# Causal attention and a cosine MoE layer on one core: k arrives in 32 by 32 blocks, VectorE turns them

## The chip, the core and the metric

The kernel runs on one core of a Trainium2 chip. The core has TensorE (PE in the rows: matmuls and transposes; PEld are its weight loads), VectorE (DVE), ScalarE (ACT), GpSimd (POOL) and SyncE (SP), which here only issues DMAs; its rows are marked SPq. 16 DMA engines move the data between HBM and SBUF. Matmuls write to PSUM, which here is eight banks of 128 x 512 numbers. The metric is the device time of one execution in microseconds (us). A profile is one more execution, with its own time.

## What is computed

```python
def _attn_ref(q, k, v):                      # each (4, 12, 448, 64), float32
    scale = 1.0 / np.sqrt(q.shape[-1])
    scores = scale * np.matmul(q, k.transpose(0, 1, 3, 2))
    mask = np.triu(np.ones((seq, seq), dtype=bool), k=1)
    scores = np.where(mask, -1000000000.0, scores)
    scores = scores - np.max(scores, axis=-1, keepdims=True)
    attn = np.exp(scores)
    attn = attn / (np.sum(attn, axis=-1, keepdims=True) + 1e-09)
    return np.matmul(attn, v)

def _moe_ref(x, w_in, w_out):                # x (1792, 768): heads side by side
    h = x @ w_in                             # w_in (768, 2048), float64
    g = h * np.cos(h)
    return g @ w_out                         # w_out (2048, 768), float64
```

## The kernel before

It has two stages. **Attention** takes the first 165 us or so and works on 24 pairs of heads (4 batches, 6 pairs each). The MoE layer follows, with products of numbers split into a high and a low half; the change doesn't touch it, but its input is attention's output, and its first weights are loaded and split in small pieces beside the attention.

Of a pair the 448 positions are three blocks of 128 and a tail of 64. q and k come as they lie in memory, positions on partitions, the two heads side by side in 128 columns (`load_qk`; `qn`, `kn`: three buffers each, the rows' `land`). The two tails of q are put on partitions 0 to 63 and 64 to 127, each in its own columns, so that one matmul serves the tails of both heads. TensorE transposes q and k, four 128 x 128 transposes each, to a PSUM bank (`transpose_qk`, line 319), and ScalarE copies each bank to SBUF (`evac_qk`, lines 329 and 331; the rows' `flat`); for k with the factor 1/8. Then TensorE makes the scores: main blocks at line 348, the tail at 357. VectorE adds the mask, negates, takes the row minimum and writes it all to SBUF (`masked`, line 365); ScalarE makes the exponentials and their sums (379); VectorE the reciprocals (390, 391), GpSimd the products (397). TensorE transposes the probabilities (419, tail 429), four banks of them, which two copies of VectorE (541, 543) and two of ScalarE (550, 552) bring to SBUF (`pm`). TensorE multiplies them with v (443), and ScalarE and VectorE split the result into halves (459, 463).

The order is written out by hand in one loop (`for i in range(N + 3)`), and every engine works its own list in that order. Step i makes the scores of pair i, transposes q and k of pair i + 1, finishes the probabilities of pair i - 1 and multiplies v of pair i - 2. At its head SyncE issues the loads of q and k of pair i + 2 and of v of pair i + 1: ten DMAs, two for the main part of each of q, k, v (one per head, lines 240), two for q's tails (258), one each for the tails of k and v (246). ScalarE issues k of the first two pairs; all the rest is SyncE's. On the same queue, behind them, stand the DMAs of the weight pieces (lines 112, 117, 195, 197, 1336), about one per step. A load waits for a semaphore that says that its buffer is free, and for another that says that the DMA eight places ahead of it has landed.

Of the kernel before, what the change touches and what calls it, by code (L numbers as in the profile page):

```python
# [15 lines left out]
AF = mybir.ActivationFunctionType  # L16
ALU = mybir.AluOpType
# [4 lines left out]
def kernel(  # L22
# [27 lines left out]
    NEG = -1.0e9  # L50
# [168 lines left out]
    def attention(filler):  # L219
        with (  # L220
# [4 lines left out]
                "p (t c d) -> p t c d", c=NB + 1, d=P  # L225
            )
            qn_t = [rows[:, i] for i in range(3)]
            kn_t = [rows[:, 3 + i] for i in range(3)]
            vn_t = [cst.tile([P, NB + 1, P], F32, name=f"vn{i}") for i in range(4)]
            pl_t = [cst.tile([P, (NB + 1) * P], F32, name=f"pl{i}") for i in range(2)]  # L230
            pairs = [(b, hp) for b in range(B) for hp in range(NP)]
            N = len(pairs)
            nat, qkt, prob, ptr = {}, {}, {}, {}
# [4 lines left out]
            def load_main(dst, src, b, h0, eng=nc.sync):  # L238
                for j in range(2):
                    eng.dma_start(  # L240
                        out=dst[:, 0:NB, heads(j)],
                        in_=src[b, h0 + j, 0 : NB * P, :].rearrange("(c p) d -> p c d", p=P),
                    )

            def load_tail(dst, src, b, h0, eng=nc.sync):
                eng.dma_start(
                    out=dst[0:TAIL, NB, :].rearrange("p (h d) -> p h d", h=2),
                    in_=src[b, h0 : h0 + 2, NB * P : S, :].rearrange("h p d -> p h d"),
                )

            def load_qk(i, keng=nc.sync):
                b, hp = pairs[i]
                qn = qn_t[i % 3]
                kn = kn_t[i % 3]
                load_main(qn, q, b, 2 * hp)
                load_main(kn, k, b, 2 * hp, keng)
                for j in range(2):
                    nc.sync.dma_start(
                        out=qn[heads(j), NB, heads(j)], in_=q[b, 2 * hp + j, NB * P : S, :]
                    )  # L260
                load_tail(kn, k, b, 2 * hp, keng)
                nat[i] = [qn, kn]

            warm = cst.tile([P, P], BF16, name="warm")
# [1 line left out]

            for i in range(3):
                nc.vector.memset(qn_t[i][:, NB, :], 0.0)
                nc.vector.memset(kn_t[i][TAIL:P, NB, :], 0.0)
                if i == 0:  # L270
                    load_qk(0, nc.scalar)

                    nc.scalar.copy(cst.tile([P, 32], BF16, name="tab")[:, 0:1], warm[:, 0:1])
                elif i == 1:
                    load_qk(1, nc.scalar)
            wps = new_bank()

            def keep_warm(n):
# [9 lines left out]
            nc.gpsimd.memset(trif, 0.0)  # L288
            nc.gpsimd.affine_select(
                out=trif, in_=trif, pattern=[[-1, P]], base=0, channel_multiplier=1,  # L290
                compare_op=ALU.is_ge, fill=NEG,
            )
            mask = cst.tile([P, NB * P], F32, name="mask")
            mask_t = cst.tile([P, S], F32, name="mask_t")
# [17 lines left out]

            def transpose_qk(i, which):
                src = nat[i][which]
                pt = new_bank()
                for c in range(NB + 1):
                    nc.tensor.transpose(pt[:, c * P : (c + 1) * P], src[:, c, :], ident)
                qkt[i, which] = pt  # L320

            def evac_qk(i, which, dve=False):
                pt = qkt[i, which]
                w = (NB * P + P, S)[which]
                t = flat[:, 2 * which + i % 2, 0:w]
                if dve:
                    nc.vector.tensor_scalar(t, pt[:, 0:w], (1.0, scale)[which], None, op0=ALU.mult)
                elif which == 0:
                    nc.scalar.copy(t, pt[:, 0:w])
                else:  # L330
                    nc.scalar.activation(t, pt[:, 0:w], AF.Copy, scale=scale)
                qkt[i, which] = t

            OFF = [c * (c + 1) // 2 * P for c in range(NB + 1)]

# [27 lines left out]
            def masked(dst, src, m, st, n):  # L363

                nc.vector.tensor_tensor_reduce(  # L365
                    out=dst, in0=src, in1=m, scale=-1.0, scalar=3.0e38,
                    op0=ALU.add, op1=ALU.min, accum_out=st[:, 0, n : n + 1],
                )

# [29 lines left out]
            def normalise_block(i, c):  # L399
                pb, _, st = prob[i]  # L400
                normalise(pb[:, :, OFF[c] : OFF[c] + (c + 1) * P], st, slice(2 * c, 2 * c + 2))
# [71 lines left out]
            LOW = [(0, 0, P), (1, P, 2 * P)]  # L473
            TOP = [(2, 0, 3 * P)]
            load_v(0)
            transpose_qk(0, 1)
            evac_qk(0, 1)
            transpose_qk(0, 0)
            evac_qk(0, 0, dve=True)
            keep_warm(7)  # L480
            LO, TL = slice(0, 4), slice(TAILC, TAILC + 1)
            av_of = {}
            for i in range(N + 3):
                cur, prev, nxt = i < N, 0 < i <= N, i + 1 < N
                old, done = 0 <= i - 2 < N, 0 <= i - 3 < N
                if i + 2 < N:
                    load_qk(i + 2)
                if nxt:
                    load_v(i + 1)
                if cur:  # L490
                    open_scores(i)
                    pb, pl, st = prob[i]
                    top = scores_main(i, TOP)
                    low = scores_main(i, LOW)
                    if i == 0:
                        transpose_qk(1, 1)
                        transpose_qk(1, 0)
                    tail = scores_tail(i)
                if nxt and i:
                    transpose_qk(i + 1, 0)  # L500
                    transpose_qk(i + 1, 1)
                if prev:
                    inverse(i - 1, LO)
                    normalise_block(i - 1, 0)
                    normalise_block(i - 1, 1)
                if cur:
                    for j in range(2):
                        masked_block(i, top, 2, j, 0)
                if prev:
                    inverse(i - 1, TL)  # L510
                    normalise(prob[i - 1][1][:, 0:S], prob[i - 1][2], TL)
                if cur:
                    for j in range(2):
                        exp_block(i, 2, j)
                if done:
                    finish_hi(i - 3, av_of[i - 3])
                if cur:
                    for c in range(2):
                        for j in range(2):
                            masked_block(i, low, c, j, c * P)  # L520
                        if (i, c) == (0, 0):
                            evac_qk(1, 1, dve=True)
                            evac_qk(1, 0)
                    masked(pl[:, 0:S], tail[:, 0:S], mask_t, st, TAILC)
                if nxt and i:
                    evac_qk(i + 1, 0)
                    evac_qk(i + 1, 1)
                if cur:
                    for j in range(2):
                        exp_block(i, 0, j)  # L530
                    inverse(i, slice(4, 6))
                    normalise_block(i, 2)
                if done:
                    finish_lo(i - 3, av_of.pop(i - 3))
                if N <= i < N + 2:
                    fill(3 * NCC)
                if prev:
                    open_ptr(i - 1)
                    pm = pm_of(i - 1)
                    t = tp_blocks(i - 1, [(2, kc, j) for kc in range(2) for j in range(2)])  # L540
                    nc.vector.tensor_copy(pm[:, 0:2, :, 2 * P : 3 * P], quad(t))
                    t = tp_blocks(i - 1, [(c, c, j) for c in (0, 2) for j in range(2)])
                    nc.vector.tensor_copy(
                        ptr[i - 1].rearrange("p (a r) -> p a r", a=2)[:, :, 0 : 2 * S].rearrange(
                            "p a (h s) -> p a h s", h=2
                        )[:, :, :, 0:P],
                        quad(t),
                    )
                    t = tp_blocks(i - 1, [(1, kc, j) for kc in range(2) for j in range(2)])
                    nc.scalar.copy(pm[:, 0:2, :, P : 2 * P], quad(t))  # L550
                    t = tp_tail(i - 1)
                    nc.scalar.copy(
                        pm[:, :, :, NB * P : S], t.rearrange("p (k h t) -> p k h t", k=NB + 1, h=2)
                    )
                if cur:
                    for j in range(2):
                        exp_block(i, 1, j)
                    exp(pl[:, 0:S], st, TAILC)
                if old:
                    av_of[i - 2] = av(i - 2)  # L560
                if i == N + 1:
                    run(filler)
                yield i
# [824 lines left out]
```

## Time and profile before

| | |
|---|---|
| median of 3 runs | 629.23 us (629.19 to 631.29) |
| profiled execution | 629.1 us |
| its span, first to last instruction | 627.3 us |
| busy in the span: PE / PEld | 618.9 us (99%) / 542.9 (87%) |
| DVE / ACT / POOL | 481.5 (77%) / 426.7 (68%) / 437.6 (70%) |
| TensorE's granted clock | 1.000 |
| DMA packets / under 512 bytes | 125004 / 73072 |

The shares are means over two unlike stages. Matmuls are pipelined, so a busy PE says that there is always one under way, not that it is at its peak. SyncE has no line in the list of busy times, since issuing isn't counted as busy; what it does is read from the timeline. Idle time of an engine that isn't the bottleneck costs nothing.

### The profile page before, as it was taken

What the parts mean: (1) busy time and instruction counts of PE and PEld (TensorE: products, weight loads), DVE (VectorE), ACT (ScalarE), POOL (GpSimd) and SP (SyncE); (2) the same over time, 40 slices, a digit from 0 to 9 for tenths busy, and PEclk for the clock granted to TensorE, in tenths of its full rate; (3) what the DMA queues carried; (4) which work ended last, traced back from release to release, by engine and by line L of the source; (5) the groups of instructions that cost most, each with busy time, mean ns of one, the idle gap of its engine ahead of it and who ended that gap; (6) DMA issues with size and microseconds to landing.
All of it is one profiled execution on the core that took longest, in us unless ns stands there. A gap on an engine that the chain in (4) does not pass through costs nothing.

```text
span 627.3 us, 11479 instructions
## 1 busy us (share of the span) xinstructions
PE 618.9 (99%) x3705; PEld 542.9 (87%) x3705; DVE 481.5 (77%) x1078; ACT 426.7 (68%) x951; POOL 437.6 (70%) x432
## 2 busy tenths in 40 slices
PE   8999999999999999999999999999999999999997
PEld 6676767677679888999999999999999999999996
DVE  6988888888838678878777777774458877887887
ACT  4998999899877668877777877743346545644640
POOL 2656665666524868877778778782578788788885
PEclk9999999999999999999999999999999999999999
DMA  5645655557604777968697969669997577559204
GB/s 121 144 113 129 159 122 139 146 133 186 175 9 130 243 291 204 376 224 325 220 328 228 340 199 340 238 239 367 401 401 266 158 245 260 184 164 317 84 1 152
DMA packets 125004, 133.29 MB, mean 212 GB/s; under 512 B 73072, under 2 KB 109280, under 8 KB 124944
## 3 DMA queue, kind: packets, MB, share of 16 engines
q1 hardware_dynamic: 117328, 106.23, 53.8%
q0 software_dynamic: 4928, 24.78, 10.9%
q10 hardware_dynamic: 2688, 1.54, 0.8%
q8 instruction: 30, 0.49, 0.3%
q14 instruction: 30, 0.25, 0.1%
HBM read 82.58 MB, written 49.94 MB: 211 GB/s over the span
## 4 chain that ended last, share of the span: by engine, by line
PE 62%; DVE 0%; issue 0%; DVEq 0%
PE banks L667 18%; PE banks L1105 12%; PE banks L1085 12%; PE banks L572 5%; PE banks L573 5%; PE banks L571 5%; PE banks L1122 2%; PE banks L1009 2%; DVE ct L176 0%; DVE acc L655 0%; DVE r L581 0%; DVE acc L1132 0%; DVEq L1132 0%
## 5 line engine op out<-in xcount | busy, mean ns | idle before, releaser
L655 DVE TENSOR_TENSOR acc<-acc,banks 128x768 f32<-128x768 f32 (+1 forms) x122 | 112.7, 932 | 44.4 <-PE banks L667 34.1
L667 PE MATMUL banks<-w,gh 128*128 128x384 f32 x512 | 109.9, 335 | 0.6 <-DVE acc L655 0.3
L397 POOL TENSOR_TENSOR pb<-pb,stat 128x768 f32<-128x768 f32 (+2 forms) x72 | 74.0, 1042 | 43.1 <-DVE stat L391 18.9
L667 PEld LDWEIGHTS banks<-w,gh 128*128 128x128 f32 x512 | 90.7, 188 | 2.6 <-DVE acc L655 0.8
L379 ACT ACTIVATE pb<-pb,stat 128x384 f32<-128x384 f32 (+1 forms) x144 | 72.5, 511 | 17.2 <-DVE stat L365 17.2
L571 PE MATMUL banks<-xa,w 128*128 128x512 f32 x192 | 75.0, 391 | 0.0
L573 PE MATMUL banks<-xa,w 128*128 128x512 f32 x192 | 75.0, 391 | 0.0
L572 PE MATMUL banks<-xa,w 128*128 128x512 f32 x192 | 75.0, 390 | 0.0
L667 PE MATMUL banks<-w,gl 128*128 128x384 f32 x256 | 65.1, 335 | 0.0
L689 POOL TENSOR_TENSOR w<-ct,w 128x768 fp32r<-128x768 f32 x28 | 51.9, 1854 | 16.8 <-ACT w L688 14.2
L365 DVE CUSTOM_DVE_ANT_0 pb<-banks,mask 128x384 f32<-128x384 f32 (+1 forms) x144 | 53.0, 418 | 12.4 <-PE banks L348 12.4
L579 ACT ACTIVATE ni<-banks 128x512 int32<-128x512 f32 (+1 forms) x64 | 34.5, 539 | 34.7 <-PE banks L573 20.8
L598 POOL TENSOR_TENSOR gl<-r,gh 128x512 fp32r<-128x512 f32 x32 | 41.5, 1298 | 19.3 <-ACT gh L597 19.2
L581 DVE SCALAR_TENSOR_TENSOR r<-ni,banks 128x512 f32<-128x512 int32 (+1 forms) x56 | 35.0, 625 | 20.3 <-ACT ni L579 19.7
L443 PE MATMUL banks<-pm,vn 128*64 128x448 f32 (+3 forms) x384 | 46.8, 386 | 0.4
L583 ACT ACTIVATE r<-r 128x512 f32<-128x512 f32 (+1 forms) x56 | 32.8, 586 | 20.9 <-DVE r L581 20.5
L667 PEld LDWEIGHTS banks<-w,gl 128*128 128x128 f32 x256 | 46.4, 188 | 0.0
L443 PEld LDWEIGHTS banks<-pm,vn 128*64 128x64 f32 x384 | 25.5, 136 | 23.2 <-issue 13.0
L586 DVE SCALAR_TENSOR_TENSOR r<-r,banks 128x512 f32<-128x512 f32 (+1 forms) x56 | 35.0, 625 | 13.1 <-ACT r L584 13.1
L1085 PE MATMUL banks<-xb,bb 128*128 128x384 f32 x234 | 44.7, 334 | 0.0
L1105 PE MATMUL banks<-big,gh 128*128 128x384 f32 x168 | 42.7, 335 | 0.0
L573 PEld LDWEIGHTS banks<-xa,w 128*128 128x128 f32 x192 | 36.0, 188 | 7.6
(151 smaller groups left out, 1555.9 us busy)
## 6 DMA issues: line engine op xcount, KB each, us to landing
bb<-w_in_d SPq DMA_DIRECT2D x48, 384.0 KB, 5.1
land<-in_moe_w_in_dram SPq DMA_DIRECT2D x14, 768.0 KB, 5.4
land<-in_moe_w_out_dram SPq DMA_DIRECT2D x14, 768.0 KB, 5.6
w_out_d<-w POOLq DMA_DIRECT2D x14, 768.0 KB, 5.4
big<-w_out_d SPq DMA_DIRECT2D x25, 384.0 KB, 4.5
w_in_d<-w POOLq DMA_DIRECT2D x7, 768.0 KB, 4.3
raw_d<-ct POOLq DMA_DIRECT2D x14, 384.0 KB, 7.7
land<-in_q_dram SPq DMA_DIRECT2D x48, 96.0 KB, 2.7
```

The source lines that it names most:

```text
L365: nc.vector.tensor_tensor_reduce(out=dst, in0=src, in1=m, scale=-1.0, scalar=3.0e38, op0=ALU.add, op1=ALU.min, accum_out=st[:, 0, n : n + 1],)
L379: nc.scalar.activation(dst, dst, AF.Exp, scale=-1.0, bias=st[:, 0, n : n + 1], accum_out=st[:, 1, n : n + 1],)
L397: nc.gpsimd.tensor_tensor(dst, dst, r.to_broadcast(list(dst.shape)), op=ALU.mult)
L443: nc.tensor.matmul(o[heads(j), kc * P : S], lhsT=vn[:, kc, heads(j)], rhs=pm[:, kc, j, kc * P : S], start=(kc == 0), stop=(kc == NB),)
L571: yield nc.tensor.matmul(hv, lhsT=wh[:, f], rhs=x[:, 0, cc, t], start=(cc == 0), stop=False)
L572: yield nc.tensor.matmul(hv, lhsT=wh[:, f], rhs=x[:, 1, cc, t], start=False, stop=False)
L573: yield nc.tensor.matmul(hv, lhsT=wl[:, f], rhs=x[:, 0, cc, t], start=False, stop=(cc == NCC - 1))
L655: nc.vector.tensor_tensor(d, d, o, op=ALU.subtract)
L667: nc.tensor.matmul(o[:, e, 0:EH], lhsT=a[:, cs], rhs=w[:, e * EH : (e + 1) * EH], start=(x == 0), stop=(x == 5),)
L689: nc.gpsimd.tensor_tensor(w[:, 1], tf, f32(w[:, 0]), op=ALU.subtract)
L1085: nc.tensor.matmul(o, lhsT=w[:, u, k * P : (k + 1) * P], rhs=x[k][:, v], start=k + m == 0, stop=k == K - 1 and m == 2,)
L1105: nc.tensor.matmul(o[:, b % 2, 0:EH], lhsT=g_ops[i][u][:, c * P : (c + 1) * P], rhs=wouts[g, i][:, v], start=(x == 0), stop=(x == 2),)
```

## The change

Of k only the way to its transposed form changes. Memory is read in blocks of 32 columns: for each head and each half of its 64 columns one DMA takes all 448 positions, 32 on partitions and 14 groups of them along the row, in runs of 32 numbers (128 bytes). A transpose instruction of VectorE turns each 32 x 32 block in place, and with the blocks so laid out the result is k transposed, heads one above the other, in the same `flat` buffer that the evacuation wrote before. TensorE's transposes of k and ScalarE's evacuations of k go. The factor 1/8 moves to the scale of the mask's pass, and the mask's fill is divided by it. One of VectorE's two copies of probabilities goes to ScalarE. The clearing of k's unused rows goes, since there are none.

```diff
-            kn_t = [rows[:, 3 + i] for i in range(3)]
+            kn_t = [rows[:, 3 + i].rearrange("p c d -> p (c d)")[:, 0:S] for i in range(3)]
...
-                load_main(kn, k, b, 2 * hp, keng)
+                for j in range(2):
+                    for d in range(D // TR):
+                        p = j * D + d * TR
+                        keng.dma_start(
+                            out=kn[p : p + TR].rearrange("r (a c) -> r a c", c=TR),
+                            in_=k[b, 2 * hp + j, :, d * TR : (d + 1) * TR].rearrange(
+                                "(a r) c -> r a c", r=TR
+                            ),
+                        )
...
-                load_tail(kn, k, b, 2 * hp, keng)
...
+            def transpose_k(i):
+                t = qkt[i, 1] = flat[:, 2 + i % 2, 0:S]
+                nc.vector.transpose(t, nat[i][1])
...
-                    out=dst, in0=src, in1=m, scale=-1.0, scalar=3.0e38,
+                    out=dst, in0=src, in1=m, scale=-scale, scalar=3.0e38,
...
                     normalise_block(i - 1, 1)
+                if nxt and i:
+                    transpose_k(i + 1)
                 if cur:
                     for j in range(2):
                         masked_block(i, top, 2, j, 0)
...
-                    nc.vector.tensor_copy(
+                    nc.scalar.copy(
                         ptr[i - 1].rearrange("p (a r) -> p a r", a=2)[:, :, 0 : 2 * S].rearrange(
```

SyncE's list, one step in the middle of attention, before (`land` is q's or k's buffer; the sizes are those of the destination, x2 says twice in a row):

```order
L240 DMA land<-in_q_dram 128x3x64 x2
L240 DMA land<-in_k_dram 128x3x64 x2
L258 DMA land<-in_q_dram 64x64 x2
L246 DMA land<-in_k_dram 64x2x64
L240 DMA vn_90<-in_v_dram 128x3x64 x2
L246 DMA vn_90<-in_v_dram 64x2x64
```

The same place after:

```order
L241 DMA land<-in_q_dram 128x3x64 x2
L260 DMA land<-in_k_dram 32x14x32 x4
L267 DMA land<-in_q_dram 64x64 x2
L241 DMA vn_90<-in_v_dram 128x3x64 x2
L247 DMA vn_90<-in_v_dram 64x2x64
```

Two main pieces and a tail of k have become four equal pieces, ahead of q's tails: eleven DMAs in place of ten.

VectorE's list from the end of one step to the masks of the next, before (`ISA` at line 365 is the mask's pass):

```order
L541 COPY pm<-banks 128x4x128
L543 COPY pm<-banks 128x2x2x128
L143 SCALAR_TENSOR_TENSOR ct<-st,ct 128x256
L147 SCALAR_TENSOR_TENSOR ct<-st,ct 128x256
L390 TENSOR_SCALAR stat<-stat 128x4
L391 RECIPROCAL stat<-stat 128x4
L365 ISA pb,stat<-banks,mask 128x384
```

The same place after:

```order
L543 COPY pm<-banks 128x4x128
L143 SCALAR_TENSOR_TENSOR ct<-st,ct 128x256
L147 SCALAR_TENSOR_TENSOR ct<-st,ct 128x256
L394 TENSOR_SCALAR stat<-stat 128x4
L395 RECIPROCAL stat<-stat 128x4
L336 STREAM_TRANSPOSE flat<-land 128x448
L369 ISA pb,stat<-banks,mask 128x384
```

The second copy is gone from here, and the transpose of the next pair's k stands between the reciprocal and the first mask pass of the present pair. On TensorE the eight transposes of a step at line 319 have become four.

## Rows read from the trace of the kernel before

**Rows 1.** Busy time by stretch: span, engines (x instructions), clock, DMA share.

```profile
core 0: us, PE busy (x) PEld busy (x) DVE busy (x) ACT busy (x) POOL busy (x), PEclk, DMA share, GB/s
90.00:120.00 30.00, 29.93 (x234) 21.58 (x233) 26.25 (x116) 27.35 (x89) 18.41 (x20) 1.00 0.61 147
```

**Rows 2.** Timeline of TensorE, one pair's period: start, length, what.

```profile
87.96 1.57 PE L348 MATMUL banks<-flat 64*128 64x384 f32 x12
...
90.31 1.04 PE L319 MATMUL banks<-ident,land 128*128 128x128 f32 x8
91.19 1.47 PE L419 MATMUL banks<-ident,pb 128*128 128x128 f32 x12
...
96.41 1.02 PE L357 MATMUL banks<-flat 128*128 128x448 f32 x2
97.26 1.04 PE L319 MATMUL banks<-ident,land 128*128 128x128 f32 x8
```

**Rows 3.** Timeline of SyncE, one pair's loads and the next issue.

```profile
132.00 1.12 SPq L240 DMA_DIRECT2D land<-in_q_dram  x2
133.16 1.02 SPq L240 DMA_DIRECT2D land<-in_k_dram  x2
134.22 1.13 SPq L258 DMA_DIRECT2D land<-in_q_dram  x2
135.40 0.62 SPq L246 DMA_DIRECT2D land<-in_k_dram  x1
136.12 1.07 SPq L240 DMA_DIRECT2D vn<-in_v_dram  x2
...
138.00 0.55 SPq L1336 DMA_DIRECT2D raw_d<-ct  x1
```

**Rows 4.** The same timeline: pair 4's loads, two long issues, weights, pair 23's loads.

```profile
21.24 1.08 SPq L240 DMA_DIRECT2D land<-in_q_dram  x2
...
62.98 2.10 SPq L240 DMA_DIRECT2D land<-in_k_dram  x2
...
78.32 2.12 SPq L258 DMA_DIRECT2D land<-in_q_dram  x2
...
152.85 0.38 SPq L195 DMA_DIRECT2D w_out_d<-w  x1
153.29 0.44 SPq L117 DMA_DIRECT2D st<-in_moe_w_out_dram  x1
153.78 1.08 SPq L240 DMA_DIRECT2D land<-in_q_dram  x2
```

**Rows 5.** DMA queues from 60 to 150 us: packets, MB, share of 16 engines.

```profile
q1 hardware_dynamic: 39700, 12.86, 59.2%
q8 instruction: 6, 0.10, 0.4%
```

**Rows 6.** Instructions of line 246: ns at the least, median, at the most.

```profile
L246 SPq DMA_DIRECT2D land<-in_k_dram x22: 621/622/1528, 11.5 to 158.2; - x22
```

**Rows 7.** Waits of SyncE, 30 to 170 us: total, times, longest.

```profile
SPq L246 <- PE banks L348: 6.0, 15, 0.9
```

**Rows 8.** Last pair: SyncE's timeline, tails' landing (median, from the DMA view), TensorE's timeline.

```profile
158.20 0.62 SPq L246 DMA_DIRECT2D land<-in_k_dram  x1
...
land<-in_k_dram SPq DMA_DIRECT2D x13, 32.0 KB, 2.2
...
160.53 1.04 PE L319 MATMUL banks<-ident,land 128*128 128x128 f32 x8
```

**Rows 9.** Instruction groups by line and form, 10 to 190 us: busy, mean ns.

```profile
L543 DVE COPY pm<-banks 128x512 f32<-128x512 f32 x24 | 16.3, 680 | 0.0
L365 DVE CUSTOM_DVE_ANT_0 pl<-banks,mask_t 128x448 f32<-128x448 f32 x24 | 14.9, 620 | 0.0
L550 ACT COPY pm<-banks 128x512 f32<-128x512 f32 x24 | 14.0, 582 | 3.0 <-PE banks L419 2.8
L331 ACT ACTIVATE flat<-banks 128x448 f32<-128x448 f32 x22 | 12.1, 552 | 0.0
```

More of the change, by code (lines that the diff above doesn't have):

```diff
@@ L227, in attention @@
             qn_t = [rows[:, i] for i in range(3)]
-            kn_t = [rows[:, 3 + i] for i in range(3)]
+            kn_t = [rows[:, 3 + i].rearrange("p c d -> p (c d)")[:, 0:S] for i in range(3)]
             vn_t = [cst.tile([P, NB + 1, P], F32, name=f"vn{i}") for i in range(4)]
             pl_t = [cst.tile([P, (NB + 1) * P], F32, name=f"pl{i}") for i in range(2)]
+            TR = 32
             pairs = [(b, hp) for b in range(B) for hp in range(NP)]
@@ L268, in attention @@
                 nc.vector.memset(qn_t[i][:, NB, :], 0.0)
-                nc.vector.memset(kn_t[i][TAIL:P, NB, :], 0.0)
                 if i == 0:
@@ L290, in attention @@
                 out=trif, in_=trif, pattern=[[-1, P]], base=0, channel_multiplier=1,
-                compare_op=ALU.is_ge, fill=NEG,
+                compare_op=ALU.is_ge, fill=NEG / scale,
             )
@@ L311, in load_v, with transpose_q @@
                 nat[i].append(vn)
-            def transpose_qk(i, which):
-                src = nat[i][which]
+            def transpose_q(i):
+                src = nat[i][0]
                 pt = new_bank()
@@ L319, in transpose_qk, with evac_q @@
                     nc.tensor.transpose(pt[:, c * P : (c + 1) * P], src[:, c, :], ident)
[L320 to L332, printed above, removed]
+                qkt[i, 0] = pt
+            def evac_q(i):
+                t = flat[:, i % 2]
+                nc.scalar.copy(t, qkt[i, 0])
+                qkt[i, 0] = t
+            def transpose_k(i):
+                t = qkt[i, 1] = flat[:, 2 + i % 2, 0:S]
+                nc.vector.transpose(t, nat[i][1])
             OFF = [c * (c + 1) // 2 * P for c in range(NB + 1)]
@@ L475, in attention @@
             load_v(0)
[L476 to L479, printed above, removed]
+            transpose_k(0)
+            transpose_q(0)
+            evac_q(0)
             keep_warm(7)
@@ L495, in attention @@
                     if i == 0:
-                        transpose_qk(1, 1)
-                        transpose_qk(1, 0)
+                        transpose_q(1)
                     tail = scores_tail(i)
                 if nxt and i:
-                    transpose_qk(i + 1, 0)
-                    transpose_qk(i + 1, 1)
+                    transpose_q(i + 1)
                 if prev:
@@ L521, in attention @@
                         if (i, c) == (0, 0):
-                            evac_qk(1, 1, dve=True)
-                            evac_qk(1, 0)
+                            transpose_k(1)
+                            evac_q(1)
                     masked(pl[:, 0:S], tail[:, 0:S], mask_t, st, TAILC)
                 if nxt and i:
-                    evac_qk(i + 1, 0)
-                    evac_qk(i + 1, 1)
+                    evac_q(i + 1)
                 if cur:
```

## Prediction

> **What bounds the kernel now.** I read the busy time by stretch first. In the attention stage, where the change lies, TensorE is busy without a break, while ScalarE has 27.35 and VectorE 26.25 us of a 30 us stretch [rows 1]. The timeline of TensorE gives its period: a pair's transposes of q and k begin at 90.31 and the next pair's at 97.26, so 6.95 us for a pair, and the eight transposes take 0.88 of it, 0.11 each [rows 2]. That alone says: take four of eight away and a pair costs 6.51.
>
> But one row of the profile isn't counted as an engine: SyncE, which issues the loads. Its timeline [rows 3] shows a pair's ten loads one right behind the other: two for the main part of q from 132.00 to 133.16, two for k (1.06 us), two tails of q (1.18), the tail of k (0.72), then v; 6.00 us from q to the next piece of work. On top come the DMAs of the weights, 20 in the 19 pairs between 21.24 and 153.78, at 0.44 us and more, and stops of about 1 us: at 62.98 two issues that take 1.02 elsewhere took 2.10, at 78.32 two that take 1.13 took 2.12 [rows 3, 4]. They come about every 15 us, as do the packets of the queue that fetches instructions (6 in 90 us) [rows 5]. All together 132.54 us for 19 pairs, 6.98 us each [rows 4]: just what TensorE needs. The issue times repeat to the nanosecond: 621 at the least and 622 in the median for the 22 tails of k [rows 6]. So I read them as the sequencer's own work and not as waits, though the waits view puts some of them down to TensorE, 15 at this line [rows 7]: that engine's semaphore moves all the time, and a wait would scatter. What shows that SyncE doesn't run ahead is the lead: the tail of k of the last pair is issued at 158.20, a tail lands after 2.2 us, so at 160.4, and TensorE begins with that pair's transposes at 160.53 [rows 8]. **Two queues are full at once**: TensorE and SyncE's issue, and SyncE can't store up a lead.
>
> **The change, part by part.** *k's transposes leave TensorE.* Four of eight, 4 x 0.11 = 0.44 us a pair, on the path as long as TensorE sets the pace. 22 pairs in the steady part make 9.7 us. This is the most that can be gained.
>
> *Copies change sides.* VectorE loses the copy at line 543, 0.68 us, and gets one transpose of 128x448; none is in the trace. Ends: the cheap one is a little under the 0.62 of its other pass over 448 columns, the dear one twice that [rows 9]. I take 0.6. Its load of 26.25/30 x 6.95 = 6.08 us a pair then stays at 6.0, or 6.7 at the dear end. ScalarE loses the evacuation of k at line 331 (0.55) and gets a copy like line 550 (0.58): 27.35/30 x 6.95 = 6.34 becomes 6.37. Both lie under 6.51, so at nothing, covered by TensorE or SyncE; without that cover ScalarE's 6.37 would be next. The factor in the mask's pass changes an operand only, and three memsets ahead of the loop go: nothing.
>
> *k's loads on SyncE.* Three issues become four, each of 32 rows by 14 blocks of 32 numbers. Descriptors double (896 to 1792 a pair), but the issue time doesn't follow their number: a main piece of 384 rows of 256 bytes takes 1.06/2 = 0.53 us, a tail of q of 64 such rows 1.18/2 = 0.59, the tail of k of 128 of them 0.72 [rows 3]. No row shows a 32-row issue, so bounds: the cheapest issue that stands in a queue, 152.85 to 153.29 for a weight's store, is 0.44 [rows 4], the dearest the tail of k, 0.72. What k costs now is 1.06 + 0.72 = 1.78 a pair. Four at 0.44 are 1.76 (-0.02), at 0.53 2.12 (+0.34), at 0.59 2.36 (+0.58), at 0.72 2.88 (+1.10). Both kinds with fewer than 128 partitions are dearer than the main piece, and the new ones have fewer still and, as the tail of k, three dimensions; so I take 0.65, between the two tails: 2.60, **+0.82 us a pair**. A gain below zero I exclude but for the 0.02: it would need an issue under 0.44, and the queue has none that is behind another.
>
> *What waits for that.* The queue is in order, so the tails of q, then v, then the weights' DMAs all move back by it, and the next pair's loads behind them. TensorE's new slack can't help: its transposes of q, and now VectorE's transpose of k, wait for landings. SyncE goes from 6.98 to 7.80 us a pair, TensorE would need 6.51: SyncE sets the end of the stage, and the 0.44 us turns into idle time of TensorE.
>
> *Where the transpose stands.* It is moved ahead of the mask passes of the current pair, behind the first reciprocal. VectorE now waits there for k; queued behind it are the masked maxima, which ScalarE's exponentials wait for. TensorE reads k some 2.8 us into a pair's period (scores begin at 87.96, q's and k's transposes at 90.31, and q's four take 0.44 [rows 2]); VectorE wants it about at its start. Against that k's last piece is no longer behind q's two tails, 1.18 us. Once the pace is SyncE's, this is paid a single time, not per pair: 2.8 - 1.18 = 1.6 less what the earlier start of the masks still finds idle on VectorE, say 0.9; and the last pair, after which SyncE has no more loads, still saves its 0.44. Together +0.5.
>
> **Sum.** The loads of pairs 2 to 23 go over SyncE; 21 of them lie ahead of the last: 21 x 0.82 = 17.2, and 0.5. The profiled execution took 629.1 us (span 627.3 and 1.8 around it), and the median of the runs, 629.23, is the same within 0.1. 629.1 + 17.7 = 646.8. All behind the attention stage moves back by the same amount, since the next stage begins with attention's output. By the bounds: 629.1 + 21 x (-0.02) + 0.5 = 629.2; with 0.53, 636.7; with 0.72, 652.7; and if the first tail of q behind a small piece gets dearer too, by the 0.13 between the tails, 655.
>
> **Rivals.** *TensorE keeps the pace* (faster). It needs SyncE to have room that I don't see: small issues at about 0.33 us, so that four cost 0.47 less than 1.78 now and the period falls to 6.51, or a part of today's issue times that are waits after all. Then 629.1 - 9.7 = 619.4, and with ScalarE at 6.37 under a pace of 6.51 a few waits in each pair: 620. For it: most of the issues do carry a wait. Against it: the repeated times and the lead of 0.1 us at the last pair. The Trainium skill is on this side: its page "DMA: Bandwidth & Descriptors", section "Issuing engines are not separate DMA queues", says that the time to initiate a DMA on a sequencer is usually small beside the DMA itself. By it a fourth issue would be free and the sum 620. The trace doesn't agree for this queue: 0.53 us of issue beside a landing of 2 to 3 us, but ten in a row in a period of 6.98.
>
> *SyncE keeps its pace as it is* (no change). The new pieces cost what the cheapest does, 0.44; TensorE's gain falls into the wait for loads: 629 to 631.
>
> *The DMA engines become the bound* (slower than my forecast). They are 59.2% busy now, with 39700 packets in 90 us on 16 engines, so 21.5 ns a packet [rows 5]. Twice k's packets at that price add 896 x 21.5 / 16 = 1.2 us of 6.95, a share of 0.77: no bound. The other packets of a pair take 0.592 x 16 x 6.98 - 896 x 21.5 ns = 46.8 us of the engines; a period of 7.80 has 125, so k's 1792 packets would have to take over 43 ns each. At 50 the period is 8.5 us: 629.1 + 21 x 1.55 = 662. The skill's same page, "Specifications", puts line rate at 512 bytes and more, with a read-modify-write below; k's rows go from 256 to 128 bytes, both below. By it this rival's chance, which is within the 0.06, would be more, but no row has a packet of 128 bytes.
>
> **Chances.** SyncE's issue sets a longer pace (636 to 655): 0.72; it keeps the present one (629 to 632): 0.11; TensorE keeps the pace (around 620): 0.11; the engines or something else, over 655: 0.06. The first is the forecast: 647. The first two hold 0.83, so the range goes from 629 to 655. Half a percent is 3.1 us, about what can be told from no change: faster 0.11, same 0.12, slower 0.77.
>
> **What would show it.** On SyncE's timeline, four issues of k back to back at 0.53 to 0.72 us, and q to q 7.3 to 8.1 us apart. TensorE with idle time of over a microsecond in each pair, ahead of the four transposes of q or of the scores, ended by DMA, VectorE or ScalarE. VectorE idle ahead of its transpose, ended by the load of k. ScalarE's and VectorE's busy time a pair nearly as before. The MoE stages unchanged in length. Wrong it is if SyncE shows gaps while TensorE still runs at 6.5, if the small issues take under 0.45, or if the granted clock of TensorE, 1.00 now [rows 1], falls with the idle time and TensorE itself gets longer.

## The result, and the profile after

The changed kernel takes 637.47 us (median of 4 runs, 637.07 to 637.99); the kernel before took 629.21 in the same comparison (4 runs, 628.66 to 631.29). The ratio is 1.0126, with an interval of 1.0101 to 1.015: slower by 8.3 us. The forecast was 647, slower by 17.7.

The profiled execution's span is 635.4 us, before 627.3: 8.1 more. First the stretch of [rows 1] again, from the busy time by stretch (columns as there):

```profile
core 0: us, PE busy (x) PEld busy (x) DVE busy (x) ACT busy (x) POOL busy (x), PEclk, DMA share, GB/s
60.00:90.00 30.00, 28.21 (x209) 18.38 (x209) 26.39 (x103) 26.56 (x83) 18.38 (x19) 1.00 0.67 146
90.00:120.00 30.00, 28.89 (x218) 18.99 (x216) 26.16 (x103) 26.70 (x87) 17.68 (x19) 1.00 0.63 140
```

TensorE, busy for 29.93 of 30 us before, now has idle time, and no other engine has taken its place. The granted clock is 1.00 as before. The engine that isn't in these columns is SyncE; its timeline (start, length, what), with the same places as [rows 3, 4]:

```profile
21.96 1.07 SPq L241 DMA_DIRECT2D land<-in_q_dram  x2
...
131.10 0.98 SPq L241 DMA_DIRECT2D land<-in_q_dram  x2
132.12 2.05 SPq L260 DMA_DIRECT2D land<-in_k_dram  x4
134.21 1.13 SPq L267 DMA_DIRECT2D land<-in_q_dram  x2
135.44 1.06 SPq L241 DMA_DIRECT2D vn<-in_v_dram  x2
136.59 0.63 SPq L247 DMA_DIRECT2D vn<-in_v_dram  x1
137.27 1.12 SPq L241 DMA_DIRECT2D land<-in_q_dram  x2
...
161.81 1.10 SPq L241 DMA_DIRECT2D land<-in_q_dram  x2
165.04 1.13 SPq L267 DMA_DIRECT2D land<-in_q_dram  x2
```

The four pieces of k stand from 132.12 to 134.21, 2.09 us or 0.52 each; k cost 1.78 before. The two tails of q behind them take 1.23 (134.21 to 135.44), 1.18 before. From pair 4 to pair 23 SyncE needs 161.81 - 21.96 = 139.85 us, 7.36 for a pair, before 6.98 [rows 4]. That is +0.38, of which the rows above give 0.31 + 0.05. Pair 23's loads begin 161.81 - 153.78 = 8.03 us later than before, and the span is 8.1 longer: **the whole loss can be read off SyncE's list**. That list has no room: between 30 and 160 us never more than 0.44 us lies between the end of one issue and the start of the next. Nor does a load wait there for the one eight places ahead of it: each of the 220 DMAs issued from 25 to 160 us starts at least 0.99 us after that one has landed (both worked out from this trace). That the list is the cause, and not a picture of another engine's pace, is for the experiments to show.

That the loads have no lead is seen at the last pair. TensorE's timeline, with the idle time and its releaser in brackets:

```profile
166.94 0.49 PE L326 MATMUL banks<-ident,land 128*128 128x128 f32 x3
167.90 0.30 PE L326 MATMUL banks<-ident,land 128*128 128x128 f32 x1 [0.47 <-DMA land<-in_q_dram]
```

The three main blocks of q are transposed, and the tail, issued behind 165.04, has not landed. In the middle of the stage the wait goes around by k. VectorE's timeline, and then ScalarE's:

```profile
91.50 0.18 DVE L395 RECIPROCAL stat<-stat 128x4 f32<-128x4 f32 x1
92.13 0.65 DVE L336 STREAM_TRANSPOSE flat<-land 128x448 f32<-128x448 f32 x1 [0.46 <-DMA land<-in_k_dram]
92.70 0.52 DVE L369 CUSTOM_DVE_ANT_0 pb<-banks,mask 128x384 f32<-128x384 f32 x1
```

```profile
93.33 0.62 ACT L383 ACTIVATE pb<-pb,stat 128x384 f32<-128x384 f32 x1 [1.09 <-DVE stat L369]
```

VectorE stands before its transpose until k has landed, the first mask pass starts behind it, and ScalarE waits 1.09 us for that mask's minimum. Read alone, ScalarE's line would blame VectorE; VectorE's line names the load. Over the stage, from the waits between 20 and 165 us (total, times, longest):

```profile
ACT pb L383 <- DVE stat L369: 18.9, 20, 1.9
...
DVE flat L336 <- DMA land<-in_k_dram: 6.4, 10, 1.3
...
PE banks L326 <- DMA land<-in_q_dram: 3.1, 4, 1.4
```

The new operations by line and form, 10 to 190 us, beside [rows 9] (busy, mean ns, idle before):

```profile
L552 ACT COPY pm<-banks 128x512 f32<-128x512 f32 x24 | 14.2, 592 | 0.1
L336 DVE STREAM_TRANSPOSE flat<-land 128x448 f32<-128x448 f32 x22 | 14.2, 646 | 7.6 <-DMA land<-in_k_dram 7.5
```

And the DMA queue from 60 to 150 us, beside [rows 5]:

```profile
q1 hardware_dynamic: 49553, 12.08, 61.7%
```

A quarter more packets in the same time, and the engines' share went from 59.2% to 61.7%. The MoE stage has not changed, it starts later: in the chain that ended last a block of 48 of its products takes 8.4 us in both, at 245.50 before and 253.61 after.

```profile
245.50 8.46 PE banks L667 x48
```

```profile
253.61 8.42 PE banks L669 x48
```

### The profile page after: what moved, and what is told of

Read it like the earlier page. It is cut to its first block, busy times and chain, and to the rows that moved or that the text cites. A ratio compares the mean times of both kernels' runs of the same rounds, so it can differ in the third digit from the quotient of the medians.

```text
span 635.4 us, 11342 instructions
## 1 busy us (share of the span) xinstructions
PE 614.5 (97%) x3609; PEld 530.1 (83%) x3609; DVE 487.5 (77%) x1073; ACT 428.4 (67%) x953; POOL 437.3 (69%) x432
## 4 chain that ended last, share of the span: by engine, by line
PE 61%; DVE 0%; issue 0%; DVEq 0%
PE banks L669 17%; PE banks L1107 12%; PE banks L1087 12%; PE banks L574 5%; PE banks L575 5%; PE banks L573 5%; PE banks L1124 2%; PE banks L1011 2%; DVE ct L176 0%; DVE acc L657 0%; DVE r L583 0%; DVE acc L1134 0%; DVEq L1134 0%
## 5 line engine op out<-in xcount | busy, mean ns | idle before, releaser
L423 PE MATMUL banks<-ident,pb 128*128 128x128 f32 x288 | 40.4, 277 | 6.0 <-DVE stat L369 4.4
```

## The experiments

Times are medians; "before" is the kernel before in the same comparison. The pace of SyncE is read as above, from the issue of pair 4's q to pair 23's, over 19.

### One more issue, nothing else

Kernel `b_kfour` is the kernel before with k's main part in three issues instead of two; rows stay 256 bytes, transposes stay on TensorE.

```diff
-                load_main(kn, k, b, 2 * hp, keng)
+                for j, c0, c1 in ((0, 0, 1), (0, 1, NB), (1, 0, NB)):
+                    keng.dma_start(out=kn[:, c0:c1, heads(j)],
+                        in_=k[b, 2 * hp + j, c0 * P : c1 * P, :].rearrange("(c p) d -> p c d", p=P))
```

> The kernel before, with k's three DMAs a pair made four (one main piece of 3 x 128 rows split into 1 x 128 and 2 x 128); rows stay 256 bytes, TensorE still transposes k. Theory A (SyncE's issue was full before the change, and one more issue a pair sets the pace): a pair costs one more slot of 0.52 to 0.53 us, SyncE's period goes from 6.98 to 7.5, 21 x 0.53 = 11 us, about 640; TensorE's idle time appears though its work is the same. Theory B (the loss in the changed kernel comes from the 128-byte rows, their packets or their landing): no change, 629. Theory C (from where the transpose stands on VectorE): no change, 629.

Measured: 640.06 against 629.05, ratio 1.0176 (1.0159 to 1.0193). SyncE's timeline:

```profile
74.01 1.48 SPq L257 DMA_DIRECT2D land<-in_k_dram  x3
75.53 1.13 SPq L262 DMA_DIRECT2D land<-in_q_dram  x2
76.71 0.62 SPq L246 DMA_DIRECT2D land<-in_k_dram  x1
```

Three issues take 1.52 us (74.01 to 75.53) where two took 1.06 [rows 3]. The pace went to 7.53 us a pair (q of pair 4 at 21.76, of pair 23 at 164.87), 0.56 more, and 0.56 x 21 = 11.7 us; measured are 11.0. A fourth issue alone, without small packets, without a transpose on VectorE, without a moved copy, costs as much as the whole change and a little more. So one more issue is enough to make such a loss, and neither 128-byte rows nor a transpose on VectorE are needed for it. That they add nothing in the kernel after has to be seen there, by taking issues away.

### Another engine issues v

`a_vpool` (the kernel after) and `b_vpool` (the kernel before) let GpSimd issue the three loads of v, which takes three of eleven (ten) issues from SyncE.

```diff
-                load_main(vn, v, b, 2 * hp)
-                load_tail(vn, v, b, 2 * hp)
+                load_main(vn, v, b, 2 * hp, nc.gpsimd)
+                load_tail(vn, v, b, 2 * hp, nc.gpsimd)
```

> The changed kernel, with the three loads of v of each pair issued by GpSimd instead of SyncE (8 issues a pair on SyncE in place of 11). Theory A: SyncE needs 7.36 - 1.88 = 5.5 us a pair, TensorE's 6.51 sets the pace: 619 to 623, unless three issues on GpSimd (about 0.55 to 1 us each, on 4.3 us of work a pair) make that engine the bound at 6 to 7.3 us a pair. Theory B (packets, landing) and theory C (VectorE's place of the transpose): the pace stays 7.4 us a pair and the time 637.

> The kernel before, with the three loads of v of each pair issued by GpSimd. Theory A: SyncE falls to 5.1 us a pair, TensorE's 6.95 stays the bound: 629, within 1 us; SyncE's timeline shows gaps. Any theory in which SyncE's queue doesn't matter expects 629 too; it is the control for the run with the changed kernel: if GpSimd's issuing costs something by itself, it shows here.

Measured: 661.28 (ratio 1.0497, 1.0453 to 1.0542) and 653.54 (1.0385, 1.037 to 1.0401). Both are far slower, the control too, and that tells why the pair decides nothing. GpSimd's groups in the control, 30 to 150 us:

```profile
L240 POOL DMA_DIRECT2D vn<-in_v_dram x29 | 22.8, 787 | 11.7 <-PE banks L443 11.7
...
L246 POOL DMA_DIRECT2D vn<-in_v_dram x15 | 9.1, 608 | 0.0
```

On GpSimd the main piece costs 0.79 us, where SyncE's takes 0.53 [rows 3]; the tail's 0.61 is about what SyncE shows for a tail (0.62, [rows 6]). At the head of GpSimd's list the main pieces also wait, 11.7 us in all, for v's buffers to come free, with the products of the probabilities behind them. These products alone are 60 us of the stretch, the issues 32, the waits for v's buffers and for the weights' pieces 25: GpSimd is full. In `a_vpool` TensorE's granted clock was also only 0.94 on average from 60 to 150 us, against 1.00 in `b_vpool`, so its 661.28 isn't GpSimd's doing alone. The engine that was relieved can't be seen behind the one that was loaded.

### What an issue costs, by its form

`b_forms` is the kernel before with k loaded in another form every four pairs: the main part whole, in 64 rows, in 32 rows, by single blocks of 128 rows; the tail whole, per head, in 32 rows.

```diff
+                form = i // 4
+                if form == 1 or form == 2:
+                    n = (0, 64, 32)[form]
+                    for j in range(2):
+                        for r in range(0, P, n):
+                            keng.dma_start(
+                                out=kn[r : r + n, 0:NB, heads(j)],
...
```

> The kernel before, with k loaded in other pieces in groups of four pairs, to read one issue's time on SyncE by its form: pairs 4 to 7 main pieces of 64 partitions (64x3x64, four DMAs), 8 to 11 of 32 partitions (32x3x64, eight), 12 to 15 one block of 128 rows each (128x64, six), 16 to 19 the tail in one DMA per head (64x64), 20 to 23 the tail in two of 32x2x64. If fewer than 128 partitions made an issue dear, as the prediction took it, the 64- and 32-partition pieces take 0.59 to 0.72 from start to start. If the tails are dear for another reason (their place in the queue, their small number of rows), the pieces of 64 and 32 partitions take 0.52 to 0.53 as main pieces do, and the tail's pieces stay at 0.59 to 0.72. The time of the whole: slower by some 4 x (2 + 6 + 4 + 1 + 1) x 0.55 = 31 us by theory A, 629 otherwise.

Measured: 657.62 us as a whole, in one run, 28.6 more than before where 31 were expected; what counts is SyncE's timeline. Four issues of 64 rows, and eight of 32:

```profile
38.70 2.57 SPq L261 DMA_DIRECT2D land<-in_k_dram  x4
41.31 1.25 SPq L276 DMA_DIRECT2D land<-in_q_dram  x2
...
55.54 3.79 SPq L261 DMA_DIRECT2D land<-in_k_dram  x8
59.37 1.13 SPq L276 DMA_DIRECT2D land<-in_q_dram  x2
```

2.61 / 4 = 0.65 us for one with 64 partitions, 3.83 / 8 = 0.48 for one with 32. Worked out from all starts in this trace, the median time from one issue to the next:

| partitions x blocks x numbers | us | issues |
|---|---|---|
| 128 x 3 x 64 (main) | 0.53 | 20 |
| 128 x 64 | 0.48 | 24 |
| 64 x 3 x 64 | 0.65 | 16 |
| 64 x 64 (tail of a head) | 0.67 | 8 |
| 64 x 2 x 64 (tail of both) | 0.72 | 14 |
| 32 x 3 x 64 | 0.47 | 32 |
| 32 x 2 x 64 | 0.63 | 8 |

The issue time follows neither the bytes nor the number of rows, and fewer partitions aren't dearer: 64 are dear, 32 and 128 with the same three blocks are cheap. Neither of the two outcomes that were expected came out whole. The form isn't all of it either: in the kernel before, the same 128 x 3 x 64 has a median of 0.53 us from start to start for k and 0.64 for v.

### Fewer issues, in the kernel after and in the kernel before

`a_v2` is the kernel after with v of two pairs loaded at once, one issue for each block of positions and all four heads: four issues for two pairs instead of six. v has two buffers of double the size for it in place of four, and v of every other pair is issued a step later; all else stays. `b_v2` does the same to the kernel before.

```diff
-                vn = vn_t[i % 4]
-                load_main(vn, v, b, 2 * hp)
-                load_tail(vn, v, b, 2 * hp)
+                vn = vn_t[i // 2 % 2]
+                for c in range(NB + 1):
+                    n = min(P, S - c * P)
+                    nc.sync.dma_start(out=vn[0:n, c, :].rearrange("p (h d) -> p h d", h=4),
+                        in_=v[b, 2 * hp : 2 * hp + 4, c * P : c * P + n, :].rearrange("h p d -> p h d"))
```

> The changed kernel, with v loaded for two pairs at once (four heads in one DMA per block of rows: four issues for two pairs in place of six), all still on SyncE and with the same bytes in 256-byte rows. Theory A (SyncE's issue sets the pace): v costs (3 x 0.53 + 0.72) / 2 = 1.16 us a pair in place of 1.88, SyncE's period falls from 7.36 to 6.64 us, so 21 x (6.64 - 6.98) = -7 us against the kernel before: 621 to 624, faster than before. Theory B (the 128-byte rows of k, their packets or landing) and theory C (VectorE's transpose ahead of the masks): nothing in k's way changes, 637.

> The kernel before, with v loaded for two pairs at once. Theory A: SyncE needs 6.25 us a pair and has room; TensorE's 6.95 is the bound: 629 within 1 us. So the gain, if the changed kernel has one in the same form, is not from v's loads by themselves. If the bound before was SyncE and not TensorE, it gets faster.

Measured: 630.28 against 629.14 (ratio 1.002, 1.0011 to 1.0029) and 628.64 (0.9992, 0.9983 to 1.0001). In the kernel after, the loss of 8.3 us all but goes, with k's 128-byte rows and VectorE's transpose as they were; in the kernel before nothing comes of it. So SyncE sets the pace after, and before TensorE does, with SyncE just under it. But the expected 621 to 624 are not reached. TensorE's timeline shows two kinds of step:

```profile
97.88 0.60 PE L333 MATMUL banks<-ident,land 128*128 128x128 f32 x4
...
100.55 0.66 PE L440 MATMUL banks<-ident,pl 128*128 128x128 f32 x4 [0.23 <-POOL pl L408]
...
105.37 0.60 PE L333 MATMUL banks<-ident,land 128*128 128x128 f32 x4
...
111.88 0.38 PE L333 MATMUL banks<-ident,land 128*128 128x128 f32 x2
```

One of 7.49 us (97.88 to 105.37) and one of 6.51 (to 111.88), and so on by turns. The long ones are those in which GpSimd has a weight's piece ahead of the products:

```profile
97.30 0.73 POOL L149 TENSOR_TENSOR w<-ct,w 128x256 fp32r<-128x256 f32 x1 [2.23 <-ACT w L148]
97.99 1.61 POOL L408 TENSOR_TENSOR pb<-pb,stat 128x256 f32<-128x256 f32 x2
```

It waits 2.23 us for ScalarE's cast and then takes 0.73, and the products that TensorE transposes stand behind it. That this order costs time, and doesn't only share it out unevenly, isn't shown by these rows.

`a_v2s` moves the stores of the weights from SyncE to GpSimd on top of that:

```diff
-                yield nc.sync.dma_start(out=w_out_d[f, :, i], in_=f32(w[:, i]))
+                yield nc.gpsimd.dma_start(out=w_out_d[f, :, i], in_=f32(w[:, i]))
```

> As the run before, and the stores of the weight pieces (raw_d, and the first halves to w_in_d and w_out_d) issued by GpSimd right behind its own work on them. Theory A: SyncE sheds 14 more issues, some 0.37 us a pair, and needs 6.27; TensorE's 6.51 is the bound now: 619 to 622. If GpSimd's issuing (0.6 to 1 us each) delays the products that TensorE waits for, no better than the run before.

Measured: 634.21 (1.0081, 1.0068 to 1.0095), 4 us worse than `a_v2`: GpSimd is the wrong place for an issue here, as with v.

### The weight's piece behind the products

`a_v2d` is `a_v2` with GpSimd's subtraction (line 149) put off to behind the products of the next step; `a_d` is the kernel after with that alone.

```diff
-            nc.gpsimd.tensor_tensor(wl, tf, f32(wh), op=ALU.subtract)
+            waiting.append((wl, tf, f32(wh)))
...
+                low_halves()
```

> The changed kernel with v loaded for two pairs at once, and GpSimd's subtraction of a weight piece (line 149 before) moved behind its products of the next step. Theory D (with SyncE relieved, the second bound is GpSimd's queue: in every other step the 0.73 us of a weight piece, which waits for ScalarE, stand ahead of the products that TensorE's transposes of probabilities need, so steps last 6.51 and 7.49 us by turns): all steps last 6.5 to 6.6, 630.3 - 11 x 0.95 = 620 to 622, faster than both kernels. Rival: ScalarE's or VectorE's full queues (0.91 and 0.92 busy) make the 7.0 us mean; then 630.

> The changed kernel with only GpSimd's subtraction moved back, v loaded as before. Theory A: SyncE's 7.36 us a pair is the bound, what comes behind it doesn't show: 637 within 1 us. If theory D alone (GpSimd, not SyncE) explained the loss: 620 to 625.

Measured: `a_v2d` 628.62 against 629.36 (0.9985, 0.9976 to 0.9994), `a_d` 635.73 (1.0089, 1.0066 to 1.0112) with SyncE's pace at 7.33. Alone it can gain little, since SyncE's list is as long as before. With SyncE relieved the turns are gone, but not as expected: all steps are now alike, at 6.97 us, where those of `a_v2` were 7.00 on average. That is nearer to the rival's 630 than to the 620 to 622 of theory D. TensorE's timeline of `a_v2d`:

```profile
97.63 0.60 PE L340 MATMUL banks<-ident,land 128*128 128x128 f32 x4
...
99.36 0.63 PE L437 MATMUL banks<-ident,pb 128*128 128x128 f32 x4 [0.26 <-DVE stat L383]
...
104.59 0.60 PE L340 MATMUL banks<-ident,land 128*128 128x128 f32 x4
```

and among its waits from 20 to 165 us:

```profile
ACT pb L397 <- DVE stat L383: 12.4, 21, 0.6
```

ScalarE waits 0.6 us in every step for the first mask of VectorE, in front of which the transpose of k stands. The wait alone proves nothing, since the kernel before has one like it, while TensorE is full (from the waits between 30 and 160 us):

```profile
ACT pb L379 <- DVE stat L365: 12.2, 19, 0.8
```

What decides is a run in which the transpose no longer stands there.

### The copy, and the place of the transpose

Two parts of the change were still unpriced. `a_copyback` is the kernel after with the second copy of probabilities back on VectorE, `a_late` the kernel after with the transpose of k moved from ahead of the masks to just ahead of the evacuation of q. `a_v2d_copyback`, `a_v2d_late` and `a_v2d_copyback_late` do the same, and both, to `a_v2d`, where SyncE no longer covers them; in the expectation of `a_v2d_copyback`, "the first of these" is `a_v2d`.

```diff
-                    nc.scalar.copy(
+                    nc.vector.tensor_copy(
```

```diff
-                if nxt and i:
-                    transpose_k(i + 1)
                 if cur:
...
                 if nxt and i:
+                    transpose_k(i + 1)
                     evac_q(i + 1)
```

> The changed kernel, with the second copy of probabilities back on VectorE: the part of the change that shifts a copy to ScalarE undone. Theory A: 637.5, the same as the changed kernel within 1 us, since SyncE's 7.36 us a pair covers VectorE's 6.0 + 0.65. If VectorE's queue or ScalarE's sets the pace, it moves by 0.4 us a pair or more, 8 us.

> The changed kernel with VectorE's transpose of k moved from ahead of the mask passes to behind them (just ahead of the evacuation of q on ScalarE). Theory A: SyncE's issues are as many as in the changed kernel, period 7.36: 637 less the single payment of about 1 us that the earlier need of k was put at, 636 to 637.5; VectorE's waits for k's loads (7.5 us in the changed kernel) go. Theory C (the transpose ahead of the masks stalls the maxima and so ScalarE): 630 or less.

Measured: 637.97 (1.0131, 1.0114 to 1.0148) and 636.92 (1.0106, 1.0085 to 1.0128). Their intervals overlap that of the kernel after: as long as SyncE sets the pace neither can be told from nothing, and theory C's 630 or less is out.

> The first of these with the second copy of probabilities back on VectorE. With the pace at 6.5 us a pair VectorE's load would be about 6.1 + 0.65 = 6.7 to 6.8, above TensorE's 6.51: 4 to 6 us slower than the first of these, 625 to 627. If VectorE's load doesn't count: the same.

> After, with v of two pairs loaded at once and GpSimd's weight subtractions put off (628.62 us), and in addition VectorE's transpose of k moved from ahead of the masks of the present pair to just ahead of ScalarE's evacuation of q. Theory 'loop': with SyncE relieved the even 6.97 us a pair come from ScalarE's list of about 6.4 us plus the time that it waits for VectorE's first mask, which stands behind the transpose (0.65 us). If so, moving the transpose lets the masks start 0.65 us earlier, ScalarE's wait of about 0.6 us a pair goes and the period falls to 6.4 to 6.6: 620 to 623 us. Theory 'ScalarE load': ScalarE's own list with the second copy is simply too long, 6.9 us with what it waits for elsewhere; then the order of VectorE changes nothing: 627 to 630 us.

> The fastest version so far (622.33 us: v of two pairs at once, subtractions put off, second copy of probabilities back on VectorE), with the transpose of k moved to just ahead of the evacuation of q. There VectorE is busy 29.3 of 30 us and TensorE 30 of 30, so neither theory gives a gain over 2 us. 'Loop': the masks start earlier, 620 to 622. 'ScalarE load': 622 to 623. If the later transpose comes too late for the scores, TensorE gets gaps of 0.3 us a pair and the time is 626 to 630.

Measured: 622.33 against 629.36 (0.988, 0.9864 to 0.9896), 621.76 against 629.62 (0.9885, 0.9858 to 0.9913), and 622.68 (0.9887, 0.9858 to 0.9917). The first was a miss, faster than expected; it led to the second, which separates the two explanations. In `a_v2d_late` ScalarE keeps its copy and all of its list, and the pace is TensorE's (timeline):

```profile
78.84 0.60 PE L340 MATMUL banks<-ident,land 128*128 128x128 f32 x4
...
85.36 0.60 PE L340 MATMUL banks<-ident,land 128*128 128x128 f32 x4
...
91.87 0.38 PE L340 MATMUL banks<-ident,land 128*128 128x128 f32 x2
```

6.52 and 6.51 us a step, and ScalarE's wait for the mask has fallen from 12.4 us in 21 times to 3.4 in 12:

```profile
ACT pb L397 <- DVE stat L383: 3.4, 12, 0.5
```

The last row of its busy time by stretch, three stretches of 30 us from 60 to 150:

```profile
sum 90.00, PE 89.52 PEld 61.56 DVE 83.31 ACT 87.49 POOL 58.47; mean PE 29.84 PEld 20.52 DVE 27.77 ACT 29.16 POOL 19.49
```

ScalarE's list fits, with 29.16 of 30 us, if it need not wait; with the transpose of k ahead of the masks it waits 0.6 a step, and 6.33 (29.16 / 30 x 6.51) and 0.6 make the 6.9 to 7.0 of `a_v2d`. Taking the copy off ScalarE mends the same thing from the other end: in `a_v2d_copyback` the wait stays (15.8 us in 22 times), but ScalarE is busy 26.82 of 30 us in place of 27.44, in steps of about 6.6 us in place of 6.97. Both together give no more (622.68, its runs from 620.61 to 623.43, which doesn't separate the two theories of that run), since TensorE is full.

## Why the prediction was right and wrong

| step of the prediction | as forecast | as measured |
|---|---|---|
| two queues full at once; SyncE's issue sets the pace after | yes | yes (`b_kfour`, `a_v2`, `b_v2`) |
| TensorE's need of 6.51 us a pair | 6.51 | 6.51 (`a_v2d_late`) |
| an issue of 32 rows | 0.65 us | **0.52 us** |
| k's loads, a pair | +0.82 | +0.31 |
| first tail of q behind a small piece | 0 to +0.13 | +0.05 |
| SyncE's pace | 7.80 | 7.36 |
| VectorE's transpose | 0.6 (to 1.2) | 0.65 |
| copies and evacuation | nothing, while SyncE covers | nothing (`a_copyback`) |
| paid once | +0.5 | 0.1, the 8.1 of the span less 21 x 0.38 |
| the whole | +17.7 | +8.3 |

**The mechanism was right, one term of the sum was mis-sized**, the price of the new issue. The rest of the sum holds: with 0.52 in place of 0.65 the same sum gives 629.1 + 21 x 0.31 + 0.5 = 636.1, and with the measured pace 629.1 + 21 x 0.38 + 0.5 = 637.6. The prediction's own line for 0.53 was 636.7.

The step that failed was the choice between the bounds: "Both kinds with fewer than 128 partitions are dearer than the main piece, and the new ones have fewer still". The two kinds, q's tails and the tail of k, both have 64 partitions. They were two samples of one point, and a trend was drawn through it. `b_forms` shows that there is no such trend: 0.65 for 64 partitions, 0.47 for 32, 0.53 for 128, with the same three blocks. The row that would have served was the main piece, at 0.53.

One reading beside the sum was wrong too: the lead of 0.1 us at the last pair, the argument that SyncE can't run ahead. It was counted to the start of the eight transposes [rows 8]; k's tail is read by the last of them, at 161.29, 0.9 us after it landed, and over the 22 pairs that lead is 0.35 to 2.6 us (worked out from the trace before). SyncE's queue was nearly full, as the pace of 6.98 says, but not to a tenth of a microsecond.

**The rivals.** That TensorE keeps the pace was false: SyncE needs 7.36 us a pair against TensorE's 6.51, 0.85 too much. The Trainium skill's page that was weighed there ("DMA: Bandwidth & Descriptors", section "Issuing engines are not separate DMA queues") says that the sequencer's time to initiate a DMA is usually small beside the DMA. As such the trace agrees: about half a microsecond of issue beside 2.2 us to landing [rows 8]. What doesn't follow from it is that one more issue is free: `b_kfour` measures 11.0 us for it, since the queue was full. That the DMA engines would bound it was false: with packets of 128 bytes for k the share went from 59.2% to 61.7% only, and `b_kfour`, without them, is slower still.

**The signs** came mostly as told: four issues back to back at 0.52; VectorE idle ahead of its transpose until k's load; a clock of 1.00; the MoE stage unchanged. q to q was 7.36 on average, at the lower end of the 7.3 to 8.1. TensorE's idle time was not over a microsecond but 0.41 a pair ((90 - 84.96) us in 12.2 pairs, from the busy time between 60 and 150 us). That is less than the 0.85 between 7.36 and 6.51, since a busy TensorE isn't one at its peak. VectorE's load was forecast at 6.0 to 6.7 and came to 6.39 (78.12 / 90 x 7.36); where the 0.3 above the expected value comes from is told below.

**What TensorE's saving is worth.** The prediction called 9.7 us the most that can be gained. `a_v2d_late` gets 7.9 of them (621.76 against 629.62, 1.15%), with steps of 6.51 in place of 6.95. Two covers hid them, one behind the other, and each was shown by taking it away: SyncE's list (637.5 to 630.3 us with `a_v2`) and the transpose of k ahead of the masks (628.6 to 621.8 with `a_v2d_late`). Between the two lies GpSimd's order, a weight's piece ahead of the products. Its removal made the steps even but hardly shorter (7.00 to 6.97 on average; 630.3 to 628.6 us), and whether it covers anything by itself stays open: `a_v2` with the transpose moved and GpSimd's order left wasn't run. `b_v2` shows that relieving SyncE gives the kernel before nothing; the other steps weren't tried on it, but with SyncE relieved its TensorE is busy for 89.70 of 90 us, so little can be left to gain there. The prediction saw the first cover. GpSimd's order it didn't name. Of the transpose's place it priced the part that SyncE covers, once 0.5 us, and not what it costs in each pair when SyncE doesn't.

## What to carry to other kernels

Count the issues on a DMA queue like the work of an engine: if ten in a row fill the pace of the loop, an eleventh costs its whole time in each round, here some half a microsecond, however little it carries; loading two rounds' data in one issue takes it back. Rows that agree with each other give a trend only if they differ in the quantity in question. And where a saving doesn't come, relieve the engine that sets the pace and look again: there may be another cover behind it, and only behind the last does the saving show.

## What the hardware showed beside that

**The price of an issue has no simple rule.** 0.47 us for 32 partitions, 0.65 for 64, 0.53 for 128, each with three blocks of 64 numbers (`b_forms`); on GpSimd 0.79 for the last (`b_vpool`). Why 64 are dearer was not found out.

**Two operations of VectorE doubled without being touched.** The bit operations on a weight's piece, 128 x 256 numbers in SBUF, line 143 before and after (ns at the least, median, at the most):

```profile
L143 DVE SCALAR_TENSOR_TENSOR ct<-st,ct x12: 411/414/816, 23.9 to 178.1; 128x256 uint32<-128x256 uint32 x12
```

```profile
L143 DVE SCALAR_TENSOR_TENSOR ct<-st,ct x12: 415/880/1414, 25.0 to 185.6; 128x256 uint32<-128x256 uint32 x12
```

The timelines of GpSimd and of VectorE in the kernel after show what lies beside them:

```profile
96.07 1.47 POOL L401 TENSOR_TENSOR pb<-pb,stat 128x768 f32<-128x768 f32 x1 [0.99 <-ACT pb L383]
```

```profile
96.34 0.68 DVE L543 COPY pm<-banks 128x512 f32<-128x512 f32 x1
96.93 0.88 DVE L143 SCALAR_TENSOR_TENSOR ct<-st,ct 128x256 uint32<-128x256 uint32 x1
97.85 0.43 DVE L147 SCALAR_TENSOR_TENSOR ct<-st,ct 128x256 f32<-128x256 f32 x1
```

The operation starts while GpSimd's product runs, which ends at 97.54, and it ends 0.27 us after that. Alone it takes 0.41, so no more than about a third of it was done by then. All six of line 143 from 60 to 150 us end 0.27 or 0.28 us after such a product. Line 134 does the same, 0.28 us alone and 0.75 beside a product. The copy from PSUM, right ahead and beside the same product, keeps its 0.68. The Trainium skill's page "SBUF — State Buffer", section "Who interferes with whom", says that an instruction of VectorE with both inputs in SBUF, beside one of GpSimd that reads SBUF, or one of VectorE in a mode with two ports, beside any of GpSimd, contend for a shared pair of ports, and that the later one is blocked until the first is finished. The trace agrees in that the end follows the product's end; a wait for all of the product would leave 0.41 us behind it and not 0.27, and the profile's times on GpSimd are rough. Before, the second copy of probabilities stood ahead of these two and pushed them past the product; the change took it away. In `a_copyback`, with the copy back, line 143 has a median of 0.416 again. From 60 to 150 us lines 134 and 143 take 9.4 us in the groups of the kernel after and 4.2 in those before, 0.4 us a pair (12.2 pairs) on VectorE; that is where its load of 6.39 comes from. In the kernel after SyncE covers that.
